# Cutting two zero regions differently over the 16 DMA engines, and writing a tail column plainly

## The chip, the core and the metric

One core of a Trainium2 chip runs one kernel. The metric is the device time of one execution in microseconds (us); lower is better. Two clocks appear. The profile counts from the start of the span. The records of single DMA packets have a clock of their own, on which the span of the kernel before begins at 10.4 us and ends at 797.9, 1.7 us after its last packet has ended at 796.2. To compare, add 10.4 to 10.7 us, by the run, to a time of the profile. Packet times and ends of engines below are on this packet clock; times in the profile views are not.

## The reference, cut to what matters

The reference is one decode step of a transformer layer, forward and backward: layer norm, attention of one token over the last W = 4096 positions of a cache of Sk = 32768, a gated feed-forward block, and the gradients of all inputs and weights.

```python
B, Sq, D = 2, 1, 512
Hq, Hkv, Sk, Dh = 32, 8, 32768, 128
W = min(4096, max(256, Sk // 4))
k = jnp.repeat(k_cache[:, :, Sk - W:, :], rep, axis=1)   # only the last W rows are read
...
_out, _vjp = jax.vjp(_f, A_x, A_k_cache, A_v_cache, ...)
_grads = _vjp(grad_out)
```

What matters here is the gradients of the two caches. They have the full shape (2, 8, 32768, 128) in bf16, and only the last 4096 of the 32768 rows differ from zero. The other 28672 rows of each of 2 x 2 x 8 = 32 blocks ("regions" below, 7.34 MB each, 235 MB in all) must be written as zeros. That writing is most of what the kernel moves: 235 of 332 MB.

## The kernel before

All zeros but the last region's come from one tile `zt` in SBUF (the core's own memory), through copies issued from GpSimd, one of the core's engines. The tile holds single bytes and the destination is seen as 4-byte numbers, so each byte read becomes four bytes written. A copy of `rows` partitions with `n` repeats writes `rows * n` packets of `ze * 4` bytes: 14,336 B for most regions, 8,192 B for those in `ZERO_SMALL`. A plain region is one copy with 128 rows and gives all 16 DMA engines the same number of packets. A region in `ZERO_PARTS` is cut into several copies, some with row counts such as 15, 12 or 2. These do not use all 16 engines, so they give some engines more packets and some fewer.

```python
ZE, ZE_SMALL, ZL = 3584, 2048, 3584
zt = const.tile([P, ZE], U8)
...
ZERO_PARTS = {6: ((4, 1), (15, 2), (2, 2), (15, 14), (12, 2), (128, 1), (16, 7)),
              12: ((4, 1), (15, 2), (2, 2), (15, 14), (12, 2), (128, 4), (16, 7)),
              17: ((4, 1), (15, 2), (2, 2), (15, 14), (12, 2), (128, 1), (16, 7)),
              21: ((4, 1), (15, 2), (2, 2), (15, 14), (12, 2), (128, 1), (16, 7)),
              24: ((3, 10), (15, 2), (3, 4), (15, 16), (12, 2), (128, 1), (16, 3))}   # one line in the file

def zero_rows(i, off, rows, n, ze):
    src = zt[0:rows * (P // rows):P // rows, 0:ze]
    nc.gpsimd.dma_start(out=zero_regions[i].bitcast(F32)[off:off + rows * n * ze].rearrange("(p k e) -> p k e", p=rows, k=n),
                        in_=src.unsqueeze(1).to_broadcast([rows, n, ze]))
    return off + rows * n * ze
...
def zero_probe(n):          # the small paired packets: two halves of a 14,336 B row per engine
    row, rows = (2 * n + 1, 2) if 0 < n < 7 else (0, 3) if n == 0 else (15, 1)
    ...
```

The first 29 regions and one column of the next are issued at the start. The rest of the zeros goes between the sixteen stores of computed gradients at the end, each of 2,048 KB. The last region is one plain copy issued from SyncE ("the last copy"), which can start only when an earlier store has landed, because it takes that store's buffer.

```python
for a in range(2):
    g0 = gq * 4 + a * 2
    nc.gpsimd.dma_start(out=dst_v[:, b, g0:g0 + 2, :, :], in_=sts[a][:])
    zeros(tail_zeros.pop(0))
    if n < 2:
        zero_probe(n * 4 + gq * 2 + a)
...
z_last = at(OFF_ST[(st_n[0] - 2) % len(OFF_ST)], [P, 2, ZL // 2], U32, "z_last")
nc.vector.memset(z_last[:, 0, :], 0)
nc.gpsimd.memset(z_last[:, 1, :], 0)
nc.sync.dma_start(out=zero_regions[31]..., in_=z_last[:]...)   # 32 packets of 14,336 B for each engine
```

## Time and profile before

| | before |
|---|---|
| time, median (lowest to highest) | 788.92 us (788.88 to 789.22, 3 runs) |
| span of the profiled run | 787.4 us |
| moved by DMA | 332.44 MB, 282.33 MB of it written to HBM |
| PE busy / DVE busy / GpSimd busy | 73% / 60% / 10% |
| packets on the GpSimd queue | 26,752 |

First, lines of the profile page of the kernel before: the span, the engines' busy time, the mean busy share of the 16 DMA engines in 40 equal slices (in tenths) with what they moved in GB/s, and the DMA queues (packets, MB, share of 16 engines' span; q0 is GpSimd's, q1 SyncE's).

```profile
span 787.4 us, 12487 instructions
PE 571.2 (73%) x5096; PEld 306.0 (39%) x5096; DVE 474.8 (60%) x1158; ACT 281.3 (36%) x404; POOL 74.9 (10%) x113
DMA  9999999999999999999999999999999999999997
GB/s 373 420 424 423 418 430 421 425 429 429 425 424 419 422 426 423 424 425 431 432 430 429 430 429 429 429 424 426 428 428 428 430 426 424 427 423 425 428 428 323
DMA packets 34282, 332.44 MB, mean 422 GB/s; under 512 B 2962, under 2 KB 2978, under 8 KB 3136
q0 software_dynamic: 26752, 261.10, 83.7%
q1 hardware_dynamic: 7456, 70.53, 35.4%
```

The row of nines says that DMA bounds the kernel: in 39 of 40 slices the engines are busy 90% or more. Only the last slice has 7. The stretches of 4 us in the tail show it larger. Each line has the stretch, its length, the busy time of PE (matrix products), PEld (their weight loads), DVE (vector), ACT (scalar) and POOL (GpSimd), the granted clock, the DMA share and GB/s. A share just above 1 comes from packets whose records overlap by some ns.

```profile
772.00:776.00 4.00, 0.00 (x0) 0.00 (x0) 0.00 (x0) 0.00 (x0) 0.00 (x0) 0.50 1.01 431
776.00:780.00 4.00, 0.00 (x0) 0.00 (x0) 0.00 (x0) 0.00 (x0) 0.00 (x0) 0.50 0.85 366
780.00:784.00 4.00, 0.00 (x0) 0.00 (x0) 0.00 (x0) 0.00 (x0) 0.00 (x0) 0.50 0.64 276
784.00:788.00 4.00, 0.00 (x0) 0.00 (x0) 0.00 (x0) 0.00 (x0) 0.00 (x0) 0.50 0.14 57
```

No compute engine works here; the DMA engines run dry one after the other. The share falls to 0.85, 0.64 and 0.14 because some engines have nothing left while the last ones still write.

**Which engine finishes when.** The profile does not number the DMA engines, but packets of one engine follow each other closely. Here are the ends of two such chains in the last copy, from the packet records (start, duration and end in ns on the packet clock, bytes, queue; 4 B is the semaphore write that closes an engine's share):

```
787457 535 787992 14336 q1        795135 535 795670 14336 q1
787989 535 788524 14336 q1        795666 535 796201 14336 q1
788520   9 788529     4 q1        796198   9 796207     4 q1
```

Each packet starts 3 or 4 ns before the one ahead of it ends, so a packet of 14,336 B costs its engine 0.532 us, in the last copy as long as it lasts, however many other engines are still at work. The left engine stops at 788.5 and the right one, the last of all, at 796.2. The sixteen ends, sorted:

```
before   787.1 788.3 788.5 788.6 | 791.4 792.6 793.5 | 795.2 795.2 795.3 795.6 795.7 795.8 795.8 795.9 796.2   mean 793.2
```

The mean is 793.2. A perfectly even split would therefore end 3.0 us earlier; that is all that can be had by moving packets, apart from idle time. Two such idle times showed in the chain of the engine that ends first: 3.2 us near 716 and 2.6 us before the last copy, both on the packet clock.

The GpSimd queue's DMA issues show the small paired packets that the change removes (copies, KB each, median us to landing):

```profile
out_dram<-zt POOLq DMA_DIRECT2D x6, 28.0 KB, 22.8
out_dram<-zt POOLq DMA_DIRECT2D x2, 7.0 KB, 20.9
```

### The profile page before, as it was taken

To read this page: it belongs to the slowest core of one execution; us is meant where nothing else is said; L and a number is where in the kernel's file an instruction comes from. 1 tells how busy PE (TensorE), PEld (TensorE's weight loads), DVE (VectorE), ACT (ScalarE), POOL (GpSimd) and SP (SyncE) were. 2 spreads that over 40 slices of the span, in tenths; PEclk is the share of its full clock that TensorE was granted. 3 is DMA by queue.
4 is the path that set the end of the run, shared out by engine and by line. 5 is a ranking of instruction groups with operands and counts; after the bars stand their busy time and mean duration, and the time that the engine had idled before them with its cause. 6 is when DMAs were issued, how large, how long until landed. Compare 5 with 4: busy or idle time off the path is not lost. (4 is left out here: it accounts for less than half of the span.)

```text
span 787.4 us, 12487 instructions
## 1 busy us (share of the span) xinstructions
PE 571.2 (73%) x5096; PEld 306.0 (39%) x5096; DVE 474.8 (60%) x1158; ACT 281.3 (36%) x404; POOL 74.9 (10%) x113
## 2 busy tenths in 40 slices
PE   3889999777687989880746877979788766688000
PEld 3645655354565645430423554434233222222000
DVE  2587999425632979780551267675535799899000
ACT  1532432124345424200201251654444367588000
POOL 4400000002000000200002001101000011221100
PEclk9998999969598889995787686975568599799555
DMA  9999999999999999999999999999999999999997
GB/s 373 420 424 423 418 430 421 425 429 429 425 424 419 422 426 423 424 425 431 432 430 429 430 429 429 429 424 426 428 428 428 430 426 424 427 423 425 428 428 323
DMA packets 34282, 332.44 MB, mean 422 GB/s; under 512 B 2962, under 2 KB 2978, under 8 KB 3136
## 3 DMA queue, kind: packets, MB, share of 16 engines
q0 software_dynamic: 26752, 261.10, 83.7%
q1 hardware_dynamic: 7456, 70.53, 35.4%
q8 instruction: 40, 0.66, 0.3%
q10 hardware_dynamic: 16, 0.01, 0.2%
q14 instruction: 18, 0.15, 0.0%
HBM read 49.30 MB, written 282.33 MB: 421 GB/s over the span
## 5 line engine op out<-in xcount | busy, mean ns | idle before, releaser
L427 DVE TENSOR_TENSOR mem<-mem,ee 128x512 bf16<-128x512 bf16 x512 | 181.0, 416 | 39.4 <-PE M_ps L438 39.3
L438 PE MATMUL M_ps<-mem 128*128 128x512 bf16 x512 | 143.4, 398 | 6.7 <-DVE mem L427 4.5
L841 PE MATMUL ps_g<-mem 128*128 128x512 bf16 x256 | 81.4, 418 | 24.2 <-DVE mem L91 21.2
L385 ACT COPY mem<-KT_ps 128x1024 bf16<-128x1024 bf16 x64 | 63.4, 1013 | 85.1 <-PE KT_ps L383 81.0
L112 POOL DMA_DIRECT2D out_dram<-zt x67 | 44.6, 800 | 510.5 <-DMA out_dram<-zt 498.0
L91 DVE CAST mem<-ps_g 128x512 bf16<-128x512 f32 x128 | 82.9, 688 | 8.4 <-ACT mem L93 5.1
L93 ACT CAST mem<-ps_g 128x512 bf16<-128x512 f32 x128 | 74.7, 586 | 32.7 <-PE ps_g L841 29.0
L383 PE MATMUL KT_ps<-ident_bf,mem 128*128 128x128 bf16 x512 | 49.7, 246 | 28.7 <-DMA mem<-in_A_k_cache_dram 25.3
L438 PEld LDWEIGHTS <-mem 128*128 128x128 bf16 x512 | 44.3, 100 | 49.3 <-issue 16.2
L259 PE MATMUL ps_tb<-ident_bf,mem 128*128 128x128 bf16 x480 | 56.0, 250 | 7.1 <-ACT mem L263 2.7
L841 PEld LDWEIGHTS <-mem 128*128 128x128 bf16 x256 | 26.5, 104 | 78.4 <-issue 65.9
L383 PEld LDWEIGHTS <-mem 128*128 128x128 bf16 x512 | 37.4, 110 | 36.5 <-DMA mem<-in_A_k_cache_dram 25.8
L93 ACT COPY mem<-ps_tb 128x512 bf16<-128x512 bf16 x44 | 25.8, 586 | 69.3 <-PE ps_tb L259 64.5
L259 PEld LDWEIGHTS <-mem 128*128 128x128 bf16 x480 | 37.5, 128 | 32.5 <-issue 31.2
L660 PE MATMUL VT_ps<-ident_bf,mem 128*128 128x128 bf16 x512 | 46.2, 238 | 2.2 <-ACT mem L93 1.1
L669 PE MATMUL dP_ps<-mem 128*128 128x512 bf16 x128 | 43.8, 430 | 4.7 <-ACT mem L93 4.7
L660 PEld LDWEIGHTS <-mem 128*128 128x128 bf16 x512 | 36.3, 106 | 27.3 <-issue 19.8
L93 ACT COPY mem<-VT_ps 128x1024 bf16<-128x1024 bf16 x31 | 31.7, 1022 | 40.5 <-PE VT_ps L660 39.3
L91 DVE COPY mem<-ps_tb 128x512 bf16<-128x512 bf16 x44 | 18.7, 424 | 42.0 <-PE ps_tb L259 40.7
L731 PE MATMUL ps_gr<-mem 2*128 2x512 bf16 (+1 forms) x78 | 33.4, 492 | 11.9 <-DVE mem L751 7.4
L91 DVE CAST mem<-ps_gr 128x512 bf16<-128x512 f32 (+1 forms) x38 | 24.8, 656 | 27.6 <-PE ps_gr L731 27.6
L91 DVE COPY mem<-VT_ps 128x1024 bf16<-128x1024 bf16 x33 | 23.1, 700 | 27.3 <-PE VT_ps L660 26.8
(232 smaller groups left out, 630.2 us busy)
## 6 DMA issues: line engine op xcount, KB each, us to landing
out_dram<-zt POOLq DMA_DIRECT2D x24, 7168.0 KB, 67.1
out_dram<-mem POOLq DMA_DIRECT2D x16, 2048.0 KB, 25.1
out_dram<-zt POOLq DMA_DIRECT2D x11, 1792.0 KB, 38.7
mem<-in_A_k_cache_dram SPq DMA_DIRECT2D x16, 1024.0 KB, 22.8
mem<-in_A_v_cache_dram SPq DMA_DIRECT2D x16, 1024.0 KB, 21.9
out_dram<-mem SPq DMA_DIRECT2D x5, 1792.0 KB, 21.9
out_dram<-zt POOLq DMA_DIRECT2D x3, 2940.0 KB, 85.7
out_dram<-mem SPq DMA_DIRECT2D x1, 7168.0 KB
```

The costliest lines, as they stand in the source:

```text
L91: nc.vector.tensor_copy(out=out, in_=in_)
L93: nc.scalar.copy(out=out, in_=in_)
L112: nc.gpsimd.dma_start(out=zero_regions[i].bitcast(F32)[off:off + rows * n * ze].rearrange("(p k e) -> p k e", p=rows, k=n), in_=src.unsque ...
L259: nc.tensor.transpose(out=ps[:, a, :], in_=src_block(a), identity=ident_bf[:])
L383: nc.tensor.transpose(out=KT_ps[:, jj, :], in_=Kt[b, g][:, u * 8 + jj, :], identity=ident_bf[:])
L385: nc.scalar.copy(out=KT[:], in_=KT_ps[:])
L427: nc.vector.tensor_tensor(out=pk[:, :, i, :].rearrange("p j (d t) -> p j d t", t=2), in0=Kb[:, j0:j0 + pk_j, :].rearrange("p j (d t) -> p ...
L438: nc.tensor.matmul(out=M_ps[:], lhsT=Vt[b, g][:, j, :], rhs=pk[:, jj, :, :].rearrange("p i d -> p (i d)"), start=(j == 0), stop=(j == NJ - 1))
L660: nc.tensor.transpose(out=VT_ps[:, jj, :], in_=Vt[b, g][:, a * 8 + jj, :], identity=ident_bf[:])
L669: nc.tensor.matmul(out=dP_ps[:, c, :], lhsT=dOpad[:, w0:w0 + P], rhs=VT[:, c * 4:(c + 1) * 4, :].rearrange("d a k -> d (a k)"), start=(i = ...
L731: nc.tensor.matmul(out=ps[:, :n], lhsT=lhsT_fn(k), rhs=rhs_fn(k), start=True, stop=True)
L841: nc.tensor.matmul(out=ps[:, a2, :], lhsT=lhs_bf[:, jp * P:(jp + 1) * P], rhs=rhs_bd[:, ap * 2 + a2, gq * 4:(gq + 1) * 4, :].rearrange("q ...
```

## The change

Its intent is to even out the sixteen ends. Region 17 becomes plain. Region 21 is cut so that three engines get ten packets more than the others, in place of a cut that gave one engine far fewer. The sixteen rows of region 30 that went out in small pieces go back into an ordinary column.

```diff
-ZERO_PARTS = {6: (...), 12: (...),
-    17: ((4, 1), (15, 2), (2, 2), (15, 14), (12, 2), (128, 1), (16, 7)),
-    21: ((4, 1), (15, 2), (2, 2), (15, 14), (12, 2), (128, 1), (16, 7)), 24: (...)}
+ZERO_PARTS = {6: (...), 12: (...),
+    21: ((7, 2), (2, 12), (6, 2), (2, 12), (15, 10), (128, 2), (16, 2)), 24: (...)}
...
-            rows, k = (16, 7) if (i, c) == (30, ZCOLS - 1) else (P, 1)
+            rows, k = (P, 1)
...
-    def zero_probe(n):
-        ... (7 lines)
...
-                    if n < 2:
-                        zero_probe(n * 4 + gq * 2 + a)
```

How packets fall to engines can be counted. The Trainium skill, "DMA: Bandwidth & Descriptors", section "Why a DMA increments its semaphore by 16 and not by 1", says that a copy issued from GpSimd which does not use all 16 engines runs on k consecutive ones from a round-robin cursor, with k the largest number up to 16 that divides the slowest dimension on both sides. Numbered from where the cursor starts (e0 to e15; which physical engine e0 is does not show), the old cut of region 21 gives 32 packets to e0 to e3, 21 to e4 and 33 to e5 to e15. The new cut gives 40 to e7, e8 and e15, 32 to e0 and 30 to the others.

More of the change, by code (lines that the diff above doesn't have):

```diff
@@ L105 @@
     ZERO_SMALL = (0, 1, 2, 3, 4, 7, 8, 9, 10, 11, 12, 13)
-    ZERO_PARTS = {6: ((4, 1), (15, 2), (2, 2), (15, 14), (12, 2), (128, 1), (16, 7)), 12: ((4, 1), (15, 2), (2, 2), (15, 14), (12, 2), (128, 4), (16, 7)), 17: ((4, 1), (15, 2), (2, 2), (15, 14), (12, 2), (128, 1), (16, 7)), 21: ((4, 1), (15, 2), (2, 2), (15, 14), (12, 2), (128, 1), (16, 7)), 24: ((3, 10), (15, 2), (3, 4), (15, 16), (12, 2), (128, 1), (16, 3))}
+    ZERO_PARTS = {6: ((4, 1), (15, 2), (2, 2), (15, 14), (12, 2), (128, 1), (16, 7)), 12: ((4, 1), (15, 2), (2, 2), (15, 14), (12, 2), (128, 4), (16, 7)), 21: ((7, 2), (2, 12), (6, 2), (2, 12), (15, 10), (128, 2), (16, 2)), 24: ((3, 10), (15, 2), (3, 4), (15, 16), (12, 2), (128, 1), (16, 3))}
     ZCOLS, N_FRONT = ZN // (P * ZE), 29
@@ L124, in zeros @@
             i, c = divmod(z_cols[0], ZCOLS)
-            rows, k = (16, 7) if (i, c) == (30, ZCOLS - 1) else (P, 1)
+            rows, k = (P, 1)
             zero_rows(i, c * P * ZE, rows, k, ZE)
             z_cols[0] += 1
-    def zero_probe(n):
-        row, rows = (2 * n + 1, 2) if 0 < n < 7 else (0, 3) if n == 0 else (15, 1)
-        for h in range(2 if rows == 1 else 1):
-            k, e = (2, ZE // 2) if rows > 1 else (1, ZE // 2)
-            off = ((ZCOLS - 1) * P + 112 + row) * ZE + h * ZE // 2
-            nc.gpsimd.dma_start(out=zero_regions[30].bitcast(F32)[off:off + rows * k * e].rearrange("(p k e) -> p k e", p=rows, k=k),
-                                in_=zt[0:rows * (P // rows):P // rows, 0:e].unsqueeze(1).to_broadcast([rows, k, e]))
     dh2_x = at(OFF_XR, [98, D], BF16, "xr")
```

## The prediction

> **What bounds the kernel now.** DMA. The row of 40 slices shows the 16 DMA engines busy 90% or more in every slice but the last (7 tenths), at 422 GB/s on average (DMA view: 332.44 MB); in the trace's packet records no engine count below 15 appears before the last 9 us. PE is 73% busy, DVE 60%, and the last DMA out of GpSimd is issued at about 730 us, so compute is not the limit. What can still be gained is unequal finishing of the 16 engines.
>
> **Who finishes when.** I chained the packet records engine by engine (the next packet starts a fixed few ns around the end of the one before). Which engines a copy of fewer than 16 parts uses is not in the trace; the Trainium skill, "DMA: Bandwidth & Descriptors", section "Why a DMA increments its semaphore by 16 and not by 1", says k consecutive engines from a round-robin cursor. Its count agrees: with k equal to the rows (4, 15, 2, 12, 3) and one 4-byte filler in place of each packet for engines left out, I get 26,752 packets on the GpSimd queue, exactly the profile's number. I number engines from the cursor's start. Last packets end (packet clock, end of kernel = 796.2):
> - e4: 787.15, although it already idled 3.2 us near 716 and 2.6 us before the last copy (all zeros, 32 packets of 14,336 B each engine)
> - e15 788.3; e7, e8 788.5
> - e0 to e2: 791.4, 792.6, 793.5
> - e5, e6 795.2; e3 795.3; e9 to e14 795.6 to 796.2
>
> So the kernel ends with e9 to e14; four engines are free 8 to 9 us earlier. A perfect split would save about 3 us.
>
> **What the change moves** (a 14,336 B packet takes 0.532 us, start to start, in the last copy; 0.529 in the GpSimd queue):
> - Region 17 becomes plain: e4 +11 packets, e5 to e15 -1.
> - Region 21: e7, e8, e15 get 40 and the others 30 (e0: 32), where e4 had 21, e5 to e15 33, e0 to e3 32.
> - Both: e4 +20 (+10.6 us), e7, e8, e15 +6 (+3.2 us), e0 0, e1 to e3 -2 (-1.1 us), e5, e6, e9 to e14 -4 (-2.1 us).
> - The small paired packets: 16 rows come back into a plain copy; e15 gets one packet more (+0.5 us), the others lose two 448 B packets (under 0.1 us). Nine issues on GpSimd fall away, and 15 in all; GpSimd is 10% busy and nothing waits for it.
>
> Bytes are unchanged; PE, DVE, ACT and SP instructions stay the same.
>
> **New ends.** e4: 787.15 + 10.6 less some 5.8 of idle that fills up, about 792; e7, e8 791.7; e15 792; e0 to e2 about 791 to 793.5; e5, e6 793.0; e9 to e14 793.5 to 794.1; e3 795.3 - 1.1 = 794.2. The end moves from 796.2 to about 794.2: 2.0 us less, all of it on the path, as the kernel ends with its last engine.
>
> **Prediction:** 788.92 - 2.0 = 786.9 us, 8 times in 10 within 786.0 to 788.3. Faster by over 2%: 0.005; within 2%: 0.99; slower by over 2%: 0.005.
>
> **What would show it.** The last slice's DMA share rises from 7 to 8 tenths, packets on the GpSimd queue fall to 26,528, the bytes stay at 332.4 MB; last ends lie within some 2.5 us instead of 9; e4 no longer idles near 716; e3 or one of e9 to e14 ends last.
>
> **What would make it wrong.** If e4 (whose packets are the irregular, slower ones) loses more than I count, the 20 packets make it last: up to 8 us slower. If I have e3 and e4 or a pair swapped, or the cursor starts elsewhere, a wrong engine gets the work.

## More of the kernel before

The timeline of SyncE's queue has the issue of the last copy (start, duration, engine, line, operation):

```profile
758.34 0.65 SPq L858 DMA_DIRECT2D out_dram<-mem  x1
```

On the packet clock this is 768.8; the first packet of the last copy starts at 770.1.

## The result, and the profile after

| | before | after |
|---|---|---|
| time, median (lowest to highest) | 788.9 (788.88 to 789.22, 4 runs) | 787.0 (786.89 to 787.18, 4 runs) |
| ratio | | 0.9975 (95%: 0.9958 to 0.9992) |
| span of the profiled run | 787.4 | 785.3 |
| mean end / last end, packet clock | 793.2 / 796.2 | 792.7 / 794.1 |

A ratio is the mean time of one kernel's fast runs over that of the other's fast runs of the same rounds, so it is not quite the ratio of the medians. The change is worth a quarter of a per cent: "same" by the threshold of 2%, yet the two sets of runs do not overlap. The same lines of the profile page, after:

```profile
span 785.3 us, 12472 instructions
PE 570.5 (73%) x5096; PEld 304.6 (39%) x5096; DVE 476.6 (61%) x1158; ACT 280.6 (36%) x404; POOL 66.3 (8%) x98
DMA  9999999999999999999999999999999999999998
GB/s 374 420 422 423 420 433 417 424 429 428 426 424 419 422 424 424 425 425 432 432 428 431 429 431 426 430 426 425 427 429 429 429 425 425 431 425 428 426 432 358
DMA packets 34058, 332.44 MB, mean 423 GB/s; under 512 B 2752, under 2 KB 2768, under 8 KB 2896
q0 software_dynamic: 26528, 261.10, 83.8%
```

The bytes are the same to the hundredth of a MB; GpSimd has 15 instructions fewer (98 against 113); the middle slices move within a few GB/s. The visible difference is the last slice: 8 tenths instead of 7, and 358 GB/s instead of 323. The stretches of the tail after the change:

```profile
772.00:776.00 4.00, 0.00 (x0) 0.00 (x0) 0.00 (x0) 0.00 (x0) 0.00 (x0) 0.50 1.01 434
776.00:780.00 4.00, 0.00 (x0) 0.00 (x0) 0.00 (x0) 0.00 (x0) 0.00 (x0) 0.50 1.00 430
780.00:784.00 4.00, 0.00 (x0) 0.00 (x0) 0.00 (x0) 0.00 (x0) 0.00 (x0) 0.50 0.48 204
784.00:788.00 4.00, 0.00 (x0) 0.00 (x0) 0.00 (x0) 0.00 (x0) 0.00 (x0) 0.59 0.00 0
```

The engines now stay full to 780 (share 1.00 where it was 0.85), which is 790.5 on the packet clock, and then stop within 3.1 us of each other. The sixteen ends:

```
after    791.0 791.6 791.7 791.8 791.9 791.9 792.6 | 792.9 793.1 | 793.3 793.3 793.4 793.4 793.6 793.6 794.1   mean 792.7
```

The spread shrank from 9.1 to 3.1 us. The last end moved by 2.1 us. Of this, 1.6 us is the distance of the last from the mean (3.0 before, 1.4 after) and 0.5 us is the mean itself. The two idle times of the leading engine, 5.8 us together, are 0.36 us of the mean when spread over 16; in the trace of after no chain shows a gap over 0.15 us past 670 us. The last copy is issued earlier too, as the store whose buffer it takes lands earlier:

```profile
755.71 0.65 SPq L848 DMA_DIRECT2D out_dram<-mem  x1
```

### The profile page after: what moved, and what is told of

It reads as the page before. It is cut to its first block, busy times and chain, and to the rows that moved or that the text cites. A ratio compares the mean times of both kernels' runs of the same rounds, so it can differ in the third digit from the quotient of the medians.

```text
span 785.3 us, 12472 instructions
## 1 busy us (share of the span) xinstructions
PE 570.5 (73%) x5096; PEld 304.6 (39%) x5096; DVE 476.6 (61%) x1158; ACT 280.6 (36%) x404; POOL 66.3 (8%) x98
## 2 busy tenths in 40 slices
DMA packets 34058, 332.44 MB, mean 423 GB/s; under 512 B 2752, under 2 KB 2768, under 8 KB 2896
## 3 DMA queue, kind: packets, MB, share of 16 engines
q0 software_dynamic: 26528, 261.10, 83.8%
## 5 line engine op out<-in xcount | busy, mean ns | idle before, releaser
L112 POOL DMA_DIRECT2D out_dram<-zt x61 | 41.5, 818 | 499.6 <-DMA out_dram<-zt 481.9
L375 PE MATMUL KT_ps<-ident_bf,mem 128*128 128x128 bf16 x512 | 47.0, 237 | 31.3 <-DMA mem<-in_A_k_cache_dram 26.4
```

Source lines behind the costliest of these rows:

```text
L375: nc.tensor.transpose(out=KT_ps[:, jj, :], in_=Kt[b, g][:, u * 8 + jj, :], identity=ident_bf[:])
```

## The experiments

**Theory.** The kernel ends with its last DMA engine. Only whole packets moved from late engines to early ones count. From the ends of before, labelled by engine, the end of any cut can be summed at 0.532 us a packet of 14,336 B. **Rival A:** the small paired packets themselves cost the time, and the gain is that they are gone. **Rival B:** the number of copies issued from GpSimd costs the time; the change has 15 fewer. A third rival, which no run was planned for, is taken up after the last run.

The first four kernels ran together on one chip, where before took 789.03 (788.85 to 789.44, 9 runs).

### The tail column alone

```diff
 # kernel before, ZERO_PARTS unchanged
-            rows, k = (16, 7) if (i, c) == (30, ZCOLS - 1) else (P, 1)
+            rows, k = (P, 1)
-                    if n < 2:
-                        zero_probe(n * 4 + gq * 2 + a)
```

> Kernel before, only the small paired packets replaced by a plain last copy of region 30 (9 issues fewer). Theory (the kernel ends with its last engine; only moving whole packets between engines counts): e9 to e14 still end last near 796.2 on the packet clock, e15 gets one packet more but ends near 788.8, so the time stays at 788.9 us (within 0.3). Rival A (the small packets themselves cost the time): 787.0. Rival B (fewer issues on the GpSimd queue, 9 of the change's 15): about 787.8.

Measured: 788.85 us (788.55 to 788.90, 5 runs), ratio 0.9996 (0.9984 to 1.0009). The last end is 795.8 and four engines still stop between 786.2 and 788.9. Rival A expected 787.0 and rival B about 787.8. All five runs lie above both, so rival A falls: without the small packets the median is lower by 0.2 us. The interval of the ratio is wider than that and reaches down to some 787.8 us.

### Region 17 alone

```diff
 # kernel before
-17: ((4, 1), (15, 2), (2, 2), (15, 14), (12, 2), (128, 1), (16, 7)),
```

> Kernel before, only region 17 made plain (6 issues fewer, small packets kept). Theory: e4 gets 11 packets more and no longer idles, ending below 793; e5 to e15 lose one packet each (0.53 us), so the end moves from 796.2 to 795.7 and the time to 788.4 us. Rival A (small packets): 788.9. Rival B (issues): about 788.2.

Measured: 788.36 us (788.15 to 788.37, 5 runs), ratio 0.9991 (0.9978 to 1.0003), last end 795.6 where 795.7 was expected. The size fits the theory; by itself it does not separate it from rival B, and its interval reaches 1.

### Region 21 alone

```diff
 # kernel before
-21: ((4, 1), (15, 2), (2, 2), (15, 14), (12, 2), (128, 1), (16, 7)),
+21: ((7, 2), (2, 12), (6, 2), (2, 12), (15, 10), (128, 2), (16, 2)),
```

> Kernel before, only region 21 cut in the new way (same number of issues, small packets kept). Theory: e9 to e14 lose 3 packets (1.6 us), e7, e8, e15 gain 7, e4 gains 9: end 794.6, time 787.3 us. Rivals A and B: 788.9, nothing that they count has changed.

Measured: 787.49 us (787.40 to 787.52, 5 runs), ratio 0.9980 (0.9967 to 0.9992), last end 794.5. This kernel has as many copies as before and keeps all small packets, and yet has most of the gain. Its queue even has more packets, 27,072 against 26,752, as more 4-byte fillers are sent. Rivals A and B expected no change.

### The same ten packets on other engines

```diff
 # kernel after
-21: ((7, 2), (2, 12), (6, 2), (2, 12), (15, 10), (128, 2), (16, 2)),
+21: ((9, 2), (2, 12), (4, 2), (2, 12), (15, 10), (128, 2), (16, 2)),
```

> Kernel after with the ten extra packets given to e9, e10 and e15 instead of e7, e8 and e15: same bytes, same number of issues and packets, two numbers changed. Theory: e9 and e10 end 10 packets (5.3 us) later than after, at 797 to 799, so the time is 789.7 to 791.7 us; e7 and e8 end near 787.5. Rivals A and B: 787.0, the same as after.

Measured: 791.47 us (791.44 to 791.66, 5 runs), ratio 1.0031 (1.0017 to 1.0044): some 4.5 us slower than after (787.0, measured in other rounds), and slower than before, which ran in the same rounds. The kernel has the same bytes, copies and packets as after (26,528 on the queue). Only two numbers differ, which shift where ten packets land. The ends:

```
wrong    789.3 789.4 | 791.3 791.4 792.1 792.1 792.8 793.1 793.1 793.4 793.6 793.8 793.8 794.4 | 798.8 798.8
```

Two engines end together at 798.8, 4.4 us after all others, as expected for e9 and e10. Two end first, at 789.3 to 789.4 instead of the expected 787.5. The trace has two engines idle from 769.3 to 772.2, waiting 2.9 us for the last copy. In before e7 and e8 end at 788.5; four packets fewer make that 786.4, and the wait makes it 789.3. Its tail in stretches of 4 us:

```profile
776.00:780.00 4.00, 0.00 (x0) 0.00 (x0) 0.00 (x0) 0.00 (x0) 0.00 (x0) 0.50 0.96 413
780.00:784.00 4.00, 0.00 (x0) 0.00 (x0) 0.00 (x0) 0.00 (x0) 0.00 (x0) 0.50 0.51 219
784.00:788.00 4.00, 0.00 (x0) 0.00 (x0) 0.00 (x0) 0.00 (x0) 0.00 (x0) 0.50 0.13 57
```

A share of 0.13 is two engines of sixteen: 57 GB/s. Bytes, packets and copies are those of after, so none of them explains the difference of 4.5 us: it lies in who gets the ten packets. It also supports the numbering of the engines: two were named as the late ones in advance, and two ended late.

The next two ran on another chip, with before at 788.84 (788.79 to 789.05, 7 runs).

### No cuts at all

```diff
 # kernel after
-ZERO_PARTS = {6: (...), 12: (...), 21: (...), 24: (...)}
+ZERO_PARTS = {}
```

> Kernel after with every region plain, so that all 16 engines get the same packets (24 issues fewer than after). Theory: e4 gets 26 packets of 14,336 B and 11 of 8,192 B more than in after (about 17 us) and ends alone at 808 to 812, 14 to 18 us after the others; time 801.5 to 805 us. Rival B (fewer issues are what pays): below 787.

Measured: 800.97 us (800.86 to 801.19, 4 runs), ratio 1.0154 (1.0138 to 1.0169). The time lies 0.5 us below the stated range; the last end, 808.1, lies inside it. Fewer copies, 24 less than after, made the kernel 14 us slower: rival B is out for good. Here every engine carries the same packets of the GpSimd queue and of the last copy, so the ends show how the engines differ. The page's rows:

```profile
DMA  9999999999999999999999999999999999999964
GB/s 373 421 421 424 419 429 422 424 431 427 427 422 419 424 424 424 427 426 433 430 429 430 431 431 429 426 427 430 430 428 429 425 426 428 428 429 426 428 284 196
```

One engine of sixteen is slow. It finished the GpSimd queue at 796.4. Nine others finished at 776.1 to 777.3 and six at 770.4 to 772.5. The last copy could be issued only when the slow engine's part of an earlier store had landed:

```profile
769.74 0.65 SPq L848 DMA_DIRECT2D out_dram<-mem  x1
```

That is 14.0 us later than in after. So fifteen engines stood idle for 4.4 to 11.2 us and ended together at 798.6 to 798.7, and the slow one ended 9.5 us later. I had expected 14 to 18 us between them. With the wait added it is 13.9 to 20.7 us (an estimate: 9.5 plus 4.4 to 11.2). The 796.4 itself overstates how late the slow engine is, as ten packets of the last copy, 5.3 us, went in between. These three levels are what the cuts answer: one engine needs far fewer packets, and six can carry some more.

Why that engine is slow stays open, but the trace shows how. Near 463, 484 and 498 us on the packet clock the 14,336 B packets of one engine, the one whose semaphore writes come last, start 0.533 to 0.565 us apart, while the others keep 0.529 to 0.531. One might suspect the 40 instruction packets of 16,384 B, each of which goes to one engine. As far as the chains can be told apart, they are not the cause: at these three places an instruction packet delays another engine.

### Eighteen packets instead of ten

```diff
 # kernel after
-21: ((7, 2), (2, 12), (6, 2), (2, 12), (15, 10), (128, 2), (16, 2)),
+21: ((7, 2), (2, 20), (6, 2), (2, 20), (15, 10), (128, 2)),
```

> Kernel after with 18 packets more instead of ten to the three engines e7, e8 and e15 (and 10 instead of 2 for e0). Theory, from the ends read in the trace of after: e15 gains 6 packets (3.2 us) on 794.1 and ends last at 797.3, e7 and e8 at 796 to 796.5, the others 1.1 us earlier than after; time 790.1 us. If more to these three were simply better: below 787.

Measured: 788.11 us (788.11 to 788.22, 4 runs), ratio 0.9991 (0.9974 to 1.0007). It is slower than after, as expected, but by 1 us and not by 3. The expectation was off by 2.0 us, more than any other. The ends show why:

```
18 more  790.5 790.6 792.0 792.1 792.3 792.4 792.5 792.6 792.6 792.6 793.1 793.3 | 794.6 795.0 795.2 795.4
```

Four engines are late, as four got more (e0, e7, e8, e15), but they end at 795.4 and not 797.3. I had added the extra packets to ends that I had labelled in the trace of after, where I took the last end, 794.1, for e15's. In that trace the labels are weak: the small packets, by which e0 to e15 can be told apart in the tail of before, are gone, and chains of engines in step can be swapped. Started from the labelled ends of before, the same sum gives 794.9 for e7 and e8, 795.2 for e15 and 794.6 to 796.7 for e0 (depending on which of the three ends 791.4, 792.6 and 793.5 is e0's), and 793.1 or less for the rest. That fits the four late ends. The mechanism stood; my reading of one trace did not. As this explanation came after the fact, the next pair of runs tests it.

### Fourteen packets, a better version

```diff
 # kernel after
-21: ((7, 2), (2, 12), (6, 2), (2, 12), (15, 10), (128, 2), (16, 2)),
+21: ((7, 2), (2, 16), (6, 2), (2, 16), (15, 10), (128, 2), (16, 1)),
```

> Kernel after with 14 packets more instead of ten to e7, e8 and e15 (and 6 instead of 2 to e0); all others one packet fewer. Computed from the ends read in the trace of before, where the small packets tell the engines apart (the same sums give 795.7 at most for the kernel with 18, which ended at 795.4): e7 and e8 end at 793.3, e15 at 793.6, e0 at 793 to 794, e9 to e14 at 793.0 to 793.6, e3 at 793.7. End 793.7 on the packet clock against 794.1 in after, time 786.5 to 786.7 us: better than after by 0.3 to 0.5. If instead the labels read in the trace of after were right (e15 last there at 794.1), e15 would end at 795.7 and the time be 788.5.

> The kernel after unchanged, on the same chip and in the same rounds: 787.0 us, 0.3 to 0.5 above the kernel with 14.

Measured on a third chip, in the same rounds (before: 789.00, 788.82 to 789.27, 9 runs): 786.58 us (786.45 to 786.65, 5 runs) with fourteen, 787.16 (787.00 to 787.27, 5 runs) for after unchanged; ratios to before 0.9969 (0.9955 to 0.9983) and 0.9976 (0.9964 to 0.9989). The two sets of runs don't overlap. Last ends: 793.6 with fourteen, where 793.7 was expected, and 794.2 for after.

```
14 more  790.7 791.0 792.1 792.4 792.5 792.8 793.0 793.0 793.0 793.1 793.1 793.1 793.2 793.4 793.6 793.6   mean 792.7
```

The result fits the labels from before and not those from after, which asked for 788.5; this kernel beats both. (The expected e0 at 793 to 794 leaves out the latest of the three ends that e0 could have in before, 793.5; the run with eighteen packets had excluded it, as e0 would have ended there at 796.7.) It has 0.9 us left between its mean and its last end.

All sums in one table, each from the ends of before and the packets moved, the last row apart (last end, packet clock):

| kernel | summed | measured |
|---|---|---|
| tail column alone | 796.1 | 795.8 |
| region 17 alone | 795.7 | 795.6 |
| region 21 alone | 794.6 | 794.5 |
| after | 794.2 | 794.1 |
| ten packets on e9, e10, e15 | 798.7 to 799.3 | 798.8 |
| eighteen packets | 795.2 to 796.7 (made afterwards) | 795.4 |
| fourteen packets | 793.7 | 793.6 |
| no cuts at all | 808 to 812 (from the ends of after) | 808.1 |

**A rival that the runs were not planned for.** The issue of the last copy moves with the result: 758.34 us in before, 755.71 in after, 755.18 with fourteen packets, 760.38 with the ten packets on other engines. Is the gain that this copy comes earlier? The traces speak against it. Only an engine that has run out of other packets waits for that copy. In before that is one engine, for 2.6 us, and it is the first to end; with the ten packets on other engines it is two, and they end first. All others are busy until that copy's packets come. And eighteen packets and region 21 alone have nearly the same issue, 756.78 and 756.72, but their last ends are 0.9 us apart, 795.4 and 794.5.

## Why the prediction was right

Time: 786.9 predicted, 787.0 measured; range 786.0 to 788.3.

- *What bounds the kernel.* Right. In every kernel the DMA share stays at 9 tenths until the tail, and the time follows the last packet.
- *Who finishes when, and the end moves with the last engine.* Right. The predicted ends form three groups: seven engines between 791 and 793.5, two at 793.0, seven between 793.5 and 794.2. Measured are seven from 791.0 to 792.6, two at 792.9 and 793.1, seven from 793.3 to 794.1. The sorted ends have no clear gaps there: the borders are drawn by the predicted counts. The last end was predicted at 794.2.
- *e4 takes the twenty packets without becoming the last.* Right, as far as the ends show: no engine ends late. The 3.2 us gap near 716 is gone. This was the step with the largest risk. In before, e4 ended first, which could as well have been read from the sixteen ends as a fast engine; the runs with plain regions show one engine that is late by 13.9 us or more (the estimate above). That this one is e4 is not shown by a label; it fits, as e4 is the engine that the cuts relieve.
- *The small packets and the nine issues bring almost nothing.* Right: 788.85 against 789.03 with them alone.
- *Last slice at 8 tenths, 26,528 packets, 332.44 MB.* All three as predicted.
- *Spread of 2.5 us.* A bit too small: 3.1 us, from 791.0 to 794.1. The prediction's own list of ends, about 791 to 794.2, gave 3.2.
- *e3 or one of e9 to e14 ends last.* Not shown either way. The trace of after does not carry the labels.

What was not right was outside the prediction: the expectation for eighteen packets, which rested on labels that the trace could not carry.

## What to carry to other kernels

Here the DMA engines are busy to the end and the time is set by the last of the sixteen. In such a kernel look at the tail: a DMA share that falls in steps over the last microseconds says how much an even split would bring (here 3.0 us, last end minus mean), and apart from idle time it is the most that moving packets can bring. Equal bytes for each engine was not an even split here; the fully plain version was 14 us slower than after, because one engine is slow. When tuning such a split, keep something in the trace that tells the engines apart, and sum in whole packets.

## What the Trainium skill lacked or had wrong

- "DMA: Bandwidth & Descriptors", section "Why a DMA increments its semaphore by 16 and not by 1": it says that all 16 engines post the +1 of a copy issued from GpSimd. The runs show more: for each engine left out of a copy the queue has one further 4-byte packet for each packet that a member carries. The trace of after has 1,952 packets of 4 bytes on the GpSimd queue: 77 copies with 16 semaphore writes each are 1,232, and the 720 left are these fillers. With them the count of the queue comes out exactly in before (26,752), after (26,528) and the six other kernels with cuts. With plain regions no engine is left out, and the 848 packets of 4 bytes are the semaphore writes alone. The rule of k consecutive engines from a cursor agrees with the ends of all kernels here.
- The same page, section "Latency and other measured facts", says that engines 7 and 15 are usually slower, with a best guess and no figure. The trace here does not number the engines, so neither the numbers nor the cause could be tested. It shows one slow engine, not two: with equal packets of the GpSimd queue and the last copy it ended at 808.1, the others together at 798.6 to 798.7 after a wait of 4.4 to 11.2 us.
- No page that I found speaks of the second level: six engines were 4 to 7 us ahead of the other nine with the same packets. Why stays open.
- The cursor seems to start at the same engine in each execution, though no trace shows it directly: before moves it by 15 in all, yet its runs on all chips lie between 788.8 and 789.4. No page that I found says that it is reset.
